# An attention and MLP kernel whose planned order is shifted by a table of 144 offsets, with five waits written out

## The chip, the cores and the metric

The kernel runs on one core of a Trainium2 chip. The metric is the device time of one execution in microseconds; several runs are made and their median is given. One more execution is recorded by the hardware profiler, and all times of single operations come from that one.

## The reference

Four layers work on x, 2048 rows of 640 numbers. Layers one and three are a local attention, layers two and four an MLP, each with its own layer norm and a residual; both attention layers share their weights, and so do both MLP layers.

```
x = x + A(layernorm(x), wqkv, wo)
x = x + B(layernorm(x), w1, b1, w2, b2)
x = x + A(layernorm(x), wqkv, wo)
x = x + B(layernorm(x), w1, b1, w2, b2)
```

A makes q, k and v for 32 heads of 20 numbers. Each position attends to itself and to the seven positions 2, 4, ... 14 before it (those before the start are masked), with a softmax over the eight, and a product with wo follows. B is a product from 640 to 1536, a gelu (tanh form) and a product back to 640. All is in float32.

## The kernel before

The rows are taken in four units of 512: even or odd positions (attention reaches only positions of the same parity), first or second half. A unit is four row tiles of 128. Two attention-and-MLP layers over four units make eight passes, numbered n = 0 to 7. The 32 heads are worked in four groups of eight heads; a group of a pass has the number G = 4n + g.

Products run on TensorE in float16. To keep float32's accuracy each operand is split into a high and a low half (the high half is a float16 copy, made by ScalarE, the low half is the rest, made by VectorE), and each product is three: high by high, high by low, low by high.

The steps of a pass, with their lines and the names that the texts use:

- Layer norm (from L520): statistics per row on VectorE (`sq`, L536 to L538), the power for 1/sqrt on GpSimd (`r`, L541), the normalized rows y on VectorE (L579), their high half on ScalarE (`yh`, L586) and low half on VectorE (`yl`, L588). They are transposed: in pass 0 on TensorE (`turn`, L468, with copies out of PSUM at L474 and L476), later by a DMA (`yT`, L593).
- qkv (L627): for each row tile t and group g one product `qkvp(n, t, g)` of 15 matmuls into one of three PSUM banks of the pool `ps`. ScalarE copies it out (`ev`, L633), and a DMA stores pairs of them (`put`, L639, 480 KB). Loads bring q, k and v of a group back in another layout (`inq`, `ink`, `inv`, L658).
- Attention of a group (L701 to L748) on VectorE: products of q and k (`qk`), sums over a head (`lg`), mask, maximum, difference (`lm`, `mx`, `sub`), the exponential on ScalarE (`e`, L716), sum and reciprocal (`s`, `rc`, `at`), products with v (`pv`) and their sums (`ad`, `o`). ScalarE makes the high half of the heads (`oh`, L746).
- Projection (L770): `wop(n, t, c)`, added to x by VectorE (`xh`, L776).
- MLP (function `mlp`, L807 to L849): hidden products `hp`, gelu, halves, output products.
- For the last units another MLP (`mlp_fast`) works with seven products of sums and differences of blocks (p1 to p7) instead of eight block products: its hidden products `hp` (L1021, one 320 KB load `c1` each, L1015) or `fp1`, gelu (L1027), sums and halves of h (`fs`, `fh`, `fl`, L1036 to L1041), products `fp` (L1084, their weights `fw` at L1067 and L1072, two loads of 160 KB), and the residual `fe` (L1103) with the store of the output (`done`, L1108). The sums of x that it needs are transposed by DMAs that ScalarE issues (`sT`, L515), and the sums of weights are prepared by `prep_sums` and `prep_late`.
- The weights of w1 and w2 are loaded once (`st`, L439, 320 KB), split (`hi` on ScalarE L413, `lo` on VectorE L414) and stored as float16 (`mw`, L454), while the first passes run. wqkv is split at the very start (`wq`, L413 and L414).

What sets the order is the class `Plan`. Every step is added with its engine, the steps it needs (`need`), what it gives (`give`), the buffers it uses (`use`) and a priority. `run` walks through the steps with an assumed duration for each, and at every point takes for each engine the step that can begin first; among equals the one of lowest priority number goes first. Buffers are handed out in the same walk, for example the three banks of `ps` and three buffers each of `c1` and `c2` (first and second kind of streamed weights). The result is one order for each engine; the program issues its instructions in that order, and an engine never overtakes. Nearly all DMAs are issued by SyncE, so they too go out in one order.

Of the kernel before, what the change touches and what calls it, by code (L numbers as in the profile page):

```python
# [14 lines left out]
S, D, H, DH, W, DIL, F = 2048, 640, 32, 20, 8, 2, 1536  # L15
# [52 lines left out]
LOP = {"sy": -460, "sa": -3}  # L68


class Plan:


# [24 lines left out]

    def add(self, eng, dur, prio, emit, need=(), give=(), use=(), table=None, move=0.0, lazy=False, spare=0.0,
            opens=0, beside=0, until=None):  # L100
        o = dict(eng=eng, dur=dur, prio=prio, emit=emit, need=need, give=give, use=use, table=table,
                 move=move, lazy=lazy, spare=spare, opens=opens, beside=beside, until=until, behind=None, ins=None, n=len(self.ops))
        self.ops.append(o)
        for u in use:
            if u not in self.users and u[0] in self.ORDERED and u not in self.line.setdefault(u[0], []):
                self.line[u[0]].append(u)
            self.users[u] = self.users.get(u, 0) + 1
# [133 lines left out]
def sliding_dilated_then_mlp_kernel(  # L241
# [245 lines left out]
    def sums_of_pairs(n, name, prio):  # L487
# [11 lines left out]
        for r in (2, 3, 0, 1):  # L499
# [12 lines left out]

            def turned(low=low, z=z, i=r % 2):
                v = tile_of(*sk)[:, :16 * HT2].rearrange("p (r c) -> p r c", c=HT2)
                nc.scalar.dma_start_transpose(v[:, 8 * z:8 * z + 8, i * P:(i + 1) * P], low().rearrange("p a c -> p (a c)"))  # L515

            dma_transpose(prio, turned, need=[("sl", n, r)], give=[("sT", n, r)], use=[hk, sk], by="act")

    def layernorm(n, prio, yk, twice):
        la, u = divmod(n, NU)  # L520
# [12 lines left out]
        for t in range(m if fast else 0):  # L533
            def stats(t=t):
                for i in range(2):
                    nc.vector.bn_stats(bn[:, t, 6 * i:6 * i + 6], x[u][:, t, i * D // 2:(i + 1) * D // 2])  # L536
                nc.vector.bn_aggr(bn[:, t, 12:14], bn[:, t, :12])
                return nc.vector.tensor_scalar_add(bn[:, t, 13:14], bn[:, t, 13:14], EPS)  # L538

            def rstd(t=t):  # L540
                nc.gpsimd.tensor_tensor(bn[:, t, 13:14], bn[:, t, 13:14], half[:, :1], op=OP.pow)  # L541

            dve(D, first(t), stats, need=[("x", la, u, t)], give=[("sq", name, t)], use=[lk], more=0.5)
            pool(0.5, prio, rstd, need=[("sq", name, t), "half"], give=[("r", name, t)], use=[lk])
        for t in range(0 if fast else m):
            act(D, prio, lambda t=t: nc.scalar.activation(junk, x[u][:, t], AF.Copy, scale=-1.0 / D,  # L546
# [313 lines left out]
    def prep_sums(j, prio):  # L860
# [5 lines left out]

        for z in range(2):
            dma(328, prio, lambda z=z: nc.sync.dma_start(parts()[0][:, z], B_w2[(j + z * HF) * P:(j + z * HF + 1) * P]),
                need=[("qkvp", N - 1, M - 1, NG - 1)], give=[("tr", j, z)], use=[key])

        def block(i):
            return parts()[0][:, i // 2, i % 2 * HD:(i % 2 + 1) * HD]
# [47 lines left out]
    def mlp_fast(at, b):  # L920
# [135 lines left out]
        for n, q in enumerate(PRODUCTS):  # L1056
            half, slot = (0, SLOT[q]) if SLOT[q] < 3 else (1, SLOT[q] - 3)
            for i in range(HF // 2):
# [17 lines left out]
                for t in range(2):  # L1076
# [14 lines left out]
                    else:  # L1091
                        prev = [p for p in PRODUCTS[:n] if BANKS[p] == BANKS[q]]
                        need += [("fe", b, prev[-1], t)] if prev else []
                    mm(6 * HD, 6, j, product, need=need, give=[("fp", b, q, i, t)], use=[wk, bk] + hks * (n in (0, NS - 1)))
            for t in range(2):
                bank = {"a": 0, "c": 2}[BANKS[q]] + t
                bk = (f"acc{bank}", (b, "a") if BANKS[q] == "a" else (b, "p2") if q == "p2" else (b, "c"))
# [91 lines left out]
```

## Time and profile before

| what | us |
| --- | --- |
| median of 3 runs | 1156.36 (1155.85 to 1156.84) |
| the profiled execution | 1155.75 |
| its span, first to last instruction | 1154.0 |
| TensorE (PE) busy | 1138.9 |
| VectorE (DVE) busy | 1067.8 |
| ScalarE (ACT) busy | 563.7 |
| GpSimd (POOL) busy | 158.1 |

The profiled execution's time is 1.75 us more than its span, and 0.61 us less than the median. Busy times of engines overlap, so they do not add up to the span. In a row of a timeline stand the start, the duration, the engine, the line, the operation with output and inputs, how many instructions are joined, and in brackets how long the engine was idle just before and what it waited for. In a row of waits stand the total, how often, and the longest. In a row of a stretch stand its bounds and length, the busy time and instructions of PE, weight loads, DVE, ACT and POOL, then the granted TensorE clock, the DMA share and GB/s. SPq rows are DMAs as SyncE issues them.

### The profile page before, as it was taken

Reading aid. Unit: us, or ns where it says so; the run is one execution under the profiler, and the core shown is the slowest. Engines: PE = TensorE matmul, PEld = TensorE weight load, DVE = VectorE, ACT = ScalarE, POOL = GpSimd, SP = SyncE. Lnnn points to the kernel's source line nnn. Section 1 sums busy time; section 2 is a strip of 40 time slices with the busy share of each in tenths; the row PEclk is TensorE's granted clock in tenths of the full one; section 3 lists DMA queues with packets and bytes.
Section 4 is the critical chain, followed back from the end, with each engine's and each line's share of the span. In section 5 each row is a group of like instructions: output and inputs, shape, how many; then the busy total and the mean of one; then the engine's idle time right before and its main releaser. Section 6 shows DMA issues by size and latency. Waiting matters only on the chain.

```text
span 1154.0 us, 17777 instructions
## 1 busy us (share of the span) xinstructions
PE 1138.9 (99%) x6952; PEld 647.5 (56%) x6952; DVE 1067.8 (93%) x1007; ACT 563.7 (49%) x985; POOL 158.1 (14%) x98
## 2 busy tenths in 40 slices
PE   8999999999999999999999999999999999999998
PEld 5444445577754565446555544556455546466786
DVE  7899999999999999999999999999998999988382
ACT  6475433645474438433636453357338342376260
POOL 1010001212111102101213001122410110200000
PEclk9999999999999999999999999999999999999999
DMA  9998999988976666846855774567678957688846
GB/s 283 286 346 252 253 352 298 283 280 272 250 215 186 196 187 162 238 160 171 193 196 177 189 216 164 192 183 178 184 232 262 318 176 212 197 205 225 222 121 188
DMA packets 256400, 256.73 MB, mean 222 GB/s; under 512 B 135916, under 2 KB 206908, under 8 KB 256316
## 3 DMA queue, kind: packets, MB, share of 16 engines
q1 hardware_dynamic: 252092, 254.55, 75.6%
q10 hardware_dynamic: 4224, 1.05, 0.5%
q8 instruction: 54, 0.88, 0.3%
q14 instruction: 30, 0.25, 0.1%
HBM read 175.64 MB, written 48.71 MB: 194 GB/s over the span
## 4 chain that ended last, share of the span: by engine, by line
PE 86%; DVE 8%; DMA 3%; issue 1%; ACT 1%; SPq 0%; DVEq 0%; ACTq 0%
PE ps L627 33%; PE ps L807 15%; PE acc L826 12%; PE ps L770 10%; PE acc L1084 6%; PE ps L1021 3%; PE acc L829 3%; PE acc L984 3%; DMA c<-mw 2%; DVE pr L701 2%; DVE sm L705 1%; DMA wq<-in_B_w_dram 1%; DVE wq L1036 1%; DVE pr L735 1%; DMA pr<-in_A_wqkv_dram 1%
## 5 line engine op out<-in xcount | busy, mean ns | idle before, releaser
L627 PE MATMUL ps<-wq,yT 128*128 128x480 f16 x1920 | 391.3, 366 | 0.6 <-DVE xf L776 0.4
L627 PEld LDWEIGHTS <-yT 128*128 128x128 f16 x1920 | 187.6, 98 | 200.9 <-DVE yT L474 0.8
L807 PE MATMUL ps<-yT,c 128*128 128x512 f16 (+1 forms) x1080 | 205.2, 344 | 0.0
L826 PE MATMUL acc<-c,act 128*128 128x512 f16 x720 | 200.2, 379 | 0.1
L701 DVE TENSOR_TENSOR pr<-qk 128x2560 f32<-128x2560 f32 (+1 forms) x44 | 176.5, 4014 | 2.1 <-DMA qk<-spill 2.0
L727 DVE TENSOR_TENSOR pr<-sm,v 128x2560 f32<-128x2560 f32 (+1 forms) x44 | 176.7, 4029 | 0.2
L705 DVE TENSOR_REDUCE sm<-pr 128x128 f32<-128x2560 f32 (+1 forms) x44 | 176.5, 4011 | 0.0
L807 PEld LDWEIGHTS <-c 128*128 128x128 f16 x1080 | 103.3, 98 | 86.3 <-DMA c<-mw 0.2
L829 PE MATMUL acc<-c,act 128*128 128x128 f16 x720 | 148.6, 219 | 0.1
L735 DVE TENSOR_TENSOR pr<-pr 128x1280 f32<-128x1280 f32 (+2 forms) x88 | 141.5, 1622 | 0.1
L633 ACT ACTIVATE ev<-ps 128x480 f32<-128x480 f32 x128 | 72.1, 564 | 139.1 <-PE ps L627 136.5
L770 PE MATMUL ps<-wo,yT 128*128 128x320 f16 x960 | 132.8, 299 | 1.2 <-ACT act L813 0.6
L563 POOL TENSOR_TENSOR ln<-ln,half 128x2 f32<-128x2 f32 (+1 forms) x30 | 65.3, 2179 | 398.8 <-ACT ln L560 398.8
L770 PEld LDWEIGHTS <-yT 128*128 128x128 f16 x960 | 93.7, 98 | 39.4 <-issue 2.0
L826 PEld LDWEIGHTS <-act 128*128 128x128 f16 x720 | 70.2, 98 | 81.3
L813 ACT ACTIVATE act<-ps,b 128x512 f32<-128x512 f32 (+1 forms) x72 | 44.1, 613 | 135.0 <-PE ps L807 125.3
L748 POOL TENSOR_TENSOR ohl<-o,ohl 128x640 f16<-128x640 f32 x24 | 43.7, 1822 | 386.5 <-DVE sm L718 123.0
L1084 PE MATMUL acc<-c,wq 128*128 128x320 f16 x630 | 93.8, 299 | 0.9 <-DVE wq L1036 0.7
L1021 PE MATMUL ps<-yT,c 128*128 128x512 f16 x360 | 80.4, 385 | 2.9 <-DMA c<-mw 2.6
L1084 PEld LDWEIGHTS <-wq 128*128 128x128 f16 x630 | 61.6, 98 | 25.6 <-DVE wq L1036 1.0
L829 PEld LDWEIGHTS <-act 128*128 128x128 f16 x720 | 68.3, 98 | 6.7 <-DVE act L818 0.3
L546 ACT ACTIVATE junk<-xf 128x640 f16<-128x640 f32 x56 | 41.0, 732 | 54.5 <-DVE xf L776 42.1
(136 smaller groups left out, 1115.6 us busy)
## 6 DMA issues: line engine op xcount, KB each, us to landing
c<-mw SPq DMA_DIRECT2D x180, 320.0 KB, 3.5
spill<-ev SPq DMA_DIRECT2D x64, 480.0 KB, 4.1
qk<-spill SPq DMA_DIRECT2D x32, 880.0 KB, 6.0
v<-spill SPq DMA_DIRECT2D x32, 880.0 KB, 4.9
c<-msp SPq DMA_DIRECT2D x36, 320.0 KB, 3.5
qk<-spill SPq DMA_DIRECT2D x32, 320.0 KB, 3.5
c<-mw SPq DMA_DIRECT2D x54, 160.0 KB, 3.0
mw<-c SPq DMA_DIRECT2D x24, 320.0 KB, 5.3
```

The source lines that it names most:

```text
L627: nc.tensor.matmul(ps, transposed(yk)[:, a * KD + k, t * P:(t + 1) * P], wq[:, b, k, g], start=j == 0, stop=j == 3 * KD - 1)
L633: act(3 * GC, -400 + n, lambda i=i, pk=pk, ek=ek: nc.scalar.activation(tile_of(*ek)[:, :, i], tile_of(*pk)[:, :3 * GC].rearrange("p (a c) ...
L701: return nc.vector.tensor_mul(pr(pk), w[:, HALO + m + t0:HALO + m + t0 + TH, None, :].to_broadcast([P, TH, W, GC]), windows(w, t0, [GC, W] ...
L705: dve(E, G - 0.7, lambda pk=pk, t0=t0: nc.vector.tensor_reduce(lg(t0, t0 + TH).rearrange("p t w h -> p (t w h)"), pr(pk).rearrange("p t w ...
L727: return nc.vector.tensor_mul(pr(vk).rearrange("p t w (h d) -> p t (w h) d", d=DH), lg(t0, t0 + TH).rearrange("p t w h -> p t (w h)")[:, : ...
L735: dve(TH * w * GC, G - 0.9, lambda vk=vk, w=w: nc.vector.tensor_add(pr(vk)[:, :, 0:w], pr(vk)[:, :, 0:w], pr(vk)[:, :, w:2 * w]), need=[la ...
L770: nc.tensor.matmul(tile_of(*pk)[:, :D // 2], transposed(yk)[:, a * KD + k, t * P:(t + 1) * P], wo[:, b, k, c * D // 2:(c + 1) * D // 2], s ...
L807: nc.tensor.matmul(tile_of(*pk)[:, :nt], tile_of(*ck)[:, a, k * P:(k + 1) * P], transposed(yk)[:, c * KD + k, t0 * P:t1 * P], start=i == 0 ...
L826: nc.tensor.matmul(acc[i], w, tile_of(*wk)[:, c, :BANK], start=e == 0 and (a, c) == PASS[0], stop=end, skip_group_check=True)
L829: nc.tensor.matmul(acc[4][:, i * P:(i + 1) * P], w, tile_of(*wk)[:, c, BANK:], start=e == 0 and i == t0 and (a, c) == PASS[0], stop=end, s ...
L1021: nc.tensor.matmul(tile_of(*pk), tile_of(*ck)[:, a, k * P:(k + 1) * P], transposed(yk)[:, c * KD + k, :], start=i == 0, stop=i == 3 * KD - 1)
L1084: nc.tensor.matmul(acc[bank][:, :HD], tile_of(*hk)[half][:, a, slot, t * P:(t + 1) * P], load()[:, z, c], start=q in FIRST and i == 0 and ...
```

## The change

The class `Plan` gets a table, NUDGE, of 144 entries. Its key is what a step gives, its value is added to the step's priority. Five waits are added: the DMA transposes of sums of x (`sT`) wait for all transposes of the normalized rows of their pass; the statistics of an attention pass wait for the normalized rows of the pass before; the loads of `prep_sums` wait for all 16 qkv products of the last pass and not for the last one alone; the buffers of h stay in use through the last but one of the seven products; and a store of the output waits for every product that adds to its block.

Lines after are the lines before plus 29 or 30 (L633 is L663, L1084 is L1114). The diff, with the table cut to the entries of the places below:

```diff
+NUDGE = {
+    ('x', 0, 0, 1): -8.7, ('x', 0, 0, 2): 162.1, ('x', 0, 0, 3): 41.6, ('sq', 0, 1): 41, ('wq', 0, 1): -266.3, ('sq', ('a', 0), 3): 184.1,
...
+    ('pv', 6, 1): -298.8, ('qk', 7, 0): 356.8, ('lg', 7, 1): 525.6, ('r', ('b', 1), 3): 74.8, ('vr', ('a', 2), 2): 73.3, ('qkvp', 2, 3, 2): -29.5,
...
+}
     def add(self, eng, dur, prio, emit, need=(), give=(), use=(), table=None, move=0.0, lazy=False, spare=0.0,
             opens=0, beside=0, until=None):
+        prio += NUDGE.get(give[0], 0.0)
...
-                nc.scalar.dma_start_transpose(v[:, 8 * z:8 * z + 8, i * P:(i + 1) * P], low().rearrange("p a c -> p (a c)"))
-
-            dma_transpose(prio, turned, need=[("sl", n, r)], give=[("sT", n, r)], use=[hk, sk], by="act")
+                return nc.scalar.dma_start_transpose(v[:, 8 * z:8 * z + 8, i * P:(i + 1) * P], low().rearrange("p a c -> p (a c)"))
+
+            dma_transpose(prio, turned, need=[("sl", n, r), *[("yT", name, t) for t in range(M)]], give=[("sT", n, r)], use=[hk, sk], by="act")
...
-            dve(D, first(t), stats, need=[("x", la, u, t)], give=[("sq", name, t)], use=[lk], more=0.5)
+            dve(D, first(t), stats, need=[("x", la, u, t)] + [("y", ("a", n - 1), t)] * (n > 0), give=[("sq", name, t)], use=[lk], more=0.5)
...
-                need=[("qkvp", N - 1, M - 1, NG - 1)], give=[("tr", j, z)], use=[key])
+                need=[("qkvp", N - 1, t, g) for t in range(M) for g in range(NG)], give=[("tr", j, z)], use=[key])
...
-                    mm(6 * HD, 6, j, product, need=need, give=[("fp", b, q, i, t)], use=[wk, bk] + hks * (n in (0, NS - 1)))
+                    mm(6 * HD, 6, j, product, need=need, give=[("fp", b, q, i, t)], use=[wk, bk] + hks * (n in (0, NS - 2, NS - 1)))
...
-                        need=[("fe", b, q, t)], give=[("done", u, i, d)])
+                        need=[("fe", b, p, t) for p in PRODUCTS if SENT[p] == SENT[q]], give=[("done", u, i, d)])
...
+    made = {}
     for o in plan.run():
         o["ins"] = o["emit"]()
+        made.update((k, o["ins"]) for k in o["give"])
+        for k in o["need"]:
+            if o["give"][0][0] == "sT" and k[0] == "yT":
+                tc.add_manual_dep(o["ins"].ins, made[k].ins.name, mybir.DependencyInfo(
+                    mybir.DependencyClass.Sync, mybir.DependencyReason.DATA), reason="order")
```

No instruction of arithmetic is added or removed; the order of the instructions differs on every engine. Three places follow.

**The start, VectorE.** Before, from the first row tile's statistics (`bn` is their buffer) to the third's; `wq` are low halves of wqkv, `y_80` and `hl_82` the first tile's normalized rows and their halves, `acc_95` a PSUM bank:

```order
L536 BN_STATS bn<-xf 128x6 x2
L537 BN_AGGR bn<-bn 128x2
L538 TENSOR_SCALAR bn<-bn 128x1
L414 SCALAR_TENSOR_TENSOR wq<-pr,wq 128x5x160
L579 TENSOR_SCALAR y_80<-xf,bn 128x640
L414 SCALAR_TENSOR_TENSOR wq<-pr,wq 128x5x160
L588 TENSOR_TENSOR hl_82<-y_80,hl_82 128x640
L414 SCALAR_TENSOR_TENSOR wq<-pr,wq 128x5x160
L474 COPY yT_70<-acc_95 128x5x128
L536 BN_STATS bn<-xf 128x6 x2
L537 BN_AGGR bn<-bn 128x2
L538 TENSOR_SCALAR bn<-bn 128x1
```

The same place now:

```order
L566 BN_STATS bn<-xf 128x6 x2
L567 BN_AGGR bn<-bn 128x2
L568 TENSOR_SCALAR bn<-bn 128x1
L566 BN_STATS bn<-xf 128x6 x2
L567 BN_AGGR bn<-bn 128x2
L568 TENSOR_SCALAR bn<-bn 128x1
L609 TENSOR_SCALAR y_80<-xf,bn 128x640
L444 SCALAR_TENSOR_TENSOR wq<-pr,wq 128x5x160
L618 TENSOR_TENSOR hl_82<-y_80,hl_82 128x640
L444 SCALAR_TENSOR_TENSOR wq<-pr,wq 128x5x160 x2
L504 COPY yT_70<-acc_95 128x5x128
```

The second row tile's statistics have moved from behind the copy of the first tile's transposed rows to ahead of the first y. SyncE loads that tile second instead of after the first three weight loads, and ScalarE makes the first tile's high half after one weight split instead of three.

**Pass 2's qkv products, ScalarE.** Before, from the evacuation of product (2, 0, 3) on; `ps_90`, `ps_91` and `ps_92` are the three banks, `c<-act` are high halves of weights of the MLP, `ohl_73` is the head copy, `sm_86` the exponential:

```order
L633 ACTIVATE ev<-ps_92 128x3x160
L633 ACTIVATE ev<-ps_90 128x3x160
L633 ACTIVATE ev<-ps_91 128x3x160
L633 ACTIVATE ev<-ps_92 128x3x160
L746 ACTIVATE ohl_73<-o_84 128x4x160
L633 ACTIVATE ev<-ps_90 128x3x160
L716 ACTIVATE sm_86<-sm_86 128x256
L413 ACTIVATE c_79<-act 128x640
L633 ACTIVATE ev<-ps_91 128x3x160
L413 ACTIVATE c_74<-act 128x640
```

Now, from the same evacuation on:

```order
L663 ACTIVATE ev<-ps_90 128x3x160
L663 ACTIVATE ev<-ps_91 128x3x160
L663 ACTIVATE ev<-ps_90 128x3x160
L443 ACTIVATE c_79<-act 128x640
L443 ACTIVATE c_74<-act 128x640
L776 ACTIVATE ohl_73<-o_84 128x4x160
L663 ACTIVATE ev<-ps_91 128x3x160
L663 ACTIVATE ev<-ps_90 128x3x160
L663 ACTIVATE ev<-ps_92 128x3x160
```

TensorE runs product (2, 3, 2) just ahead of (2, 0, 3), seven products earlier; it fills bank 92, which is evacuated only at the end of these rows. The evacuation of (2, 3, 0), the fourth of the rows before, now stands behind the splits c_79 and c_74 and the head copy. On SyncE the loads of these two splits have moved ahead of a load of v (880 KB), a `put` of 480 KB and a weight store of 320 KB, and the second of them ahead of one more `put`.

**Where the products of the last tiles mix, SyncE.** Before, from the load of `c1` number 84 on (`mw_108`; number 85 is `mw_114`, 86 is `mw_109`); the rows of 128x2x320 are half-blocks `fw`:

```order
L1015 DMA c_75<-mw_108 128x1280
L1072 DMA c_79<-mw_126 128x2x320
L1072 DMA c_79<-mw_127 128x2x320
L1015 DMA c_74<-mw_114 128x1280
L658 DMA v_69<-spill_147 128x1760
L1108 DMA out_dram<-xf 128x320 x2
L1072 DMA c_77<-mw_130 128x2x320
L1072 DMA c_77<-mw_131 128x2x320
L1015 DMA c_75<-mw_109 128x1280
L1108 DMA out_dram<-xf 128x320
```

Now:

```order
L1045 DMA c_75<-mw_108 128x1280
L1045 DMA c_74<-mw_114 128x1280
L688 DMA v_69<-spill_147 128x1760
L1138 DMA out_dram<-xf 128x320 x2
L1045 DMA c_76<-mw_109 128x1280
L1138 DMA out_dram<-xf 128x320
L1102 DMA c_77<-mw_126 128x2x320
L1102 DMA c_77<-mw_127 128x2x320
```

Load 86 (`mw_109`) has moved ahead of four half-blocks, and it goes into buffer c_76 instead of c_75. On TensorE the last two p3 products of the unit, which use c_76 before it, run ahead of hidden product 84 instead of behind it, and the last p4 product runs behind hidden product 85.

More of the change, by code (lines that the diff above doesn't have):

```diff
@@ L68 @@
 LOP = {"sy": -460, "sa": -3}
+NUDGE = {
[8 rows of a table added]
+    ('qkvp', 3, 3, 2): 31.2, ('qkvp', 3, 3, 3): 7.9, ('wop', 3, 3, 0): -748.4, ('qkvp', 4, 2, 0): -50.2, ('at', 18): 4.2, ('ad', 18, 0, 4): 266.2,
[8 rows of a table added]
+    ('sr', 3, 1): 292.5, ('out', 0, 3, 1): 52.4, ('hp', 4): 646.6, ('outh', 0, 0, 3): 31.8, ('out', 0, 3, 3): 2.5, ('outh', 0, 5, 2): 104.4,
+    ('outh', 0, 5, 3): 92.5, ('out', 0, 6, 2): 3.3, ('hp', 19): 8.3, ('outh', 0, 8, 3): 2.2, ('outh', 1, 4, 1): 2.1, ('out', 1, 11, 3): -176.9,
+    ('out', 2, 11, 1): 12.2, ('outh', 3, 0, 0): 234.1, ('outh', 3, 3, 3): 379.3, ('outh', 3, 9, 3): 417.2, ('xr', 3, 0): -142.9, ('x', 1, 3, 0): -137.5,
+    ('x', 1, 3, 1): -154.6, ('hlo', 64): 75.8, ('outh', 4, 6, 2): 30.3, ('out', 4, 8, 1): 3.5, ('out', 4, 8, 3): 0.6, ('hp', 69): 1.4, ('hp', 70): 0.7,
[4 rows of a table added]
+}
 class Plan:
```

18 rows, old and new, of the table NUDGE are left out of this document.

## Prediction

> **What bounds the kernel now.** I read the page's busy times and its chain first, then TensorE by stretches, then TensorE's waits, then the single rows at three places.
>
> ```profile
> PE 1138.9 (99%) x6952; PEld 647.5 (56%) x6952; DVE 1067.8 (93%) x1007; ACT 563.7 (49%) x985; POOL 158.1 (14%) x98
> PE 86%; DVE 8%; DMA 3%; issue 1%; ACT 1%; SPq 0%; DVEq 0%; ACTq 0%
> ```
>
> TensorE is busy for 1138.9 of 1154.0 us and the chain runs through it for 86%. The change adds and removes no matmul, so all that it can give is in the 15.1 us of idle time and in matmuls that run slowly; all that it can take is a new idle time. By stretches (length, then TensorE's busy time, with the granted clock and GB/s at the end of a row):
>
> ```profile
> 0.00:20.00 20.00, 14.33 (x128) 10.25 (x129) 13.31 (x31) 10.32 (x14) 3.02 (x12) 1.00 1.01 306
> 180.00:900.00 720.00, 718.16 (x4389) 400.47 (x4388) 702.44 (x559) 361.07 (x651) 125.51 (x66) 1.00 0.72 210
> 950.00:975.00 25.00, 24.34 (x177) 17.03 (x176) 24.58 (x27) 6.79 (x9) 1.40 (x1) 1.00 0.67 191
> 975.00:1000.00 25.00, 22.16 (x125) 12.40 (x124) 24.68 (x23) 4.66 (x6) 6.65 (x1) 0.93 0.73 216
> 1070.00:1090.00 20.00, 19.57 (x162) 15.49 (x160) 5.60 (x13) 4.38 (x11) 0.00 (x0) 1.00 0.88 255
> 1130.00:1154.00 24.00, 20.68 (x153) 14.68 (x150) 4.91 (x10) 0.00 (x0) 0.00 (x0) 0.98 0.55 162
> ```
>
> The idle time is 5.67 us in the first 20, 2.84 in 975 to 1000, 3.32 in the last 24 (the end, which the change leaves nearly as it is), and only 1.84 us in the 720 us between 180 and 900. So there is little to win in the middle, and three places matter. The waits behind these holes (total, times, longest):
>
> ```profile
> PE acc L468 <- ACT hl L586: 3.0, 2, 2.0
> PE ps L1021 <- DMA c<-mw: 2.6, 1, 2.6
> PE acc L468 <- DVE hl L588: 1.2, 3, 0.6
> PE acc L1084 <- DVE wq L1036: 0.7, 1, 0.7
> PE ps L1021 <- ACT ev L1027: 0.3, 1, 0.3
> PE acc L1084 <- DVE xf L1103: 0.3, 1, 0.3
> ```
>
> **The start.** TensorE, then VectorE:
>
> ```profile
> 9.79 0.45 PE L468 MATMUL acc<-ident,hl 128*128 128x128 f16 x5 [2.02 <-ACT hl L586]
> 11.04 3.72 PE L627 MATMUL ps<-wq,yT 128*128 128x480 f16 x15
> 15.69 0.45 PE L468 MATMUL acc<-ident,hl 128*128 128x128 f16 x5 [0.94 <-ACT hl L586]
> 16.71 0.73 PE L468 MATMUL acc<-ident,hl 128*128 128x128 f16 x10 [0.57 <-DVE hl L588]
> 17.67 0.45 PE L468 MATMUL acc<-ident,hl 128*128 128x128 f16 x5 [0.23 <-DVE hl L588]
> ...
> 11.81 0.87 DVE L536 BATCH_NORM_STATS2 bn<-xf 128x6 f32<-128x320 f32 x2
> 13.03 0.88 DVE L536 BATCH_NORM_STATS2 bn<-xf 128x6 f32<-128x320 f32 x2
> 14.26 0.60 DVE L579 TENSOR_SCALAR y<-xf,bn 128x640 f32<-128x640 f32 x1
> ```
>
> After the first product TensorE waits 0.94 + 0.57 + 0.23 = 1.74 us for the second and third row tiles to be normalized. VectorE makes the statistics of both only after the first tile's transposed copy: 11.81 to 13.03 for the second, then the third, then y at 14.26. The change loads the second tile ahead of the first weights and makes its statistics before the first y, when VectorE waits for weights anyway. So 13.03 − 11.81 = 1.22 us leave the chain to y. Nothing else there is shortened, so I take **−1.2**. The bounds are −1.74 (all three waits) and 0: the tile's load now stands ahead of the weight loads of the first product.
>
> **A held PSUM bank at 130 to 157 us.** ScalarE's rows, one stretch with its GB/s, TensorE's row, and the sizes of the loads:
>
> ```profile
> 144.77 0.74 ACT L746 ACTIVATE ohl<-o 128x640 f16<-128x640 f32 x1 [0.89 <-DVE o L739]
> 146.34 0.57 ACT L633 ACTIVATE ev<-ps 128x480 f32<-128x480 f32 x1 [0.83 <-PE ps L627]
> 152.69 0.74 ACT L413 ACTIVATE c<-act 128x640 f16<-128x640 f32 x1 [3.91 <-DMA act<-in_B_w_dram]
> 155.11 0.74 ACT L413 ACTIVATE c<-act 128x640 f16<-128x640 f32 x1 [1.22 <-DMA act<-in_B_w_dram]
> ...
> 143.80:155.10 11.30, 11.30 (x58) 5.48 (x56) 8.90 (x10) 3.00 (x6) 1.40 (x1) 1.00 1.07 345
> ...
> 127.66 32.56 PE L627 MATMUL ps<-wq,yT 128*128 128x480 f16 x160
> ...
> spill<-ev SPq DMA_DIRECT2D x64, 480.0 KB, 4.1
> v<-spill SPq DMA_DIRECT2D x32, 880.0 KB, 4.9
> mw<-c SPq DMA_DIRECT2D x24, 320.0 KB, 5.3
> ```
>
> A qkv product is 15 matmuls, 32.56 × 15 / 160 = 3.05 us; none waits here before. After the change the product (2,3,2) runs 21 us early and keeps one of the three banks until its evacuation, which still stands late on ScalarE. TensorE then alternates between two banks, so product (2,3,1) can start only when the evacuation of (2,3,0) is done. That one has moved behind two weight splits and the head copy (ohl). The product that the row at 146.34 evacuates has just ended; one more of 3.05 us fits, so (2,3,1) is due at 149.2, or 148.0 with the start's 1.2. The second of the two splits ran at 155.11 when its weights landed. In the new order of SyncE a store of 480 KB, the load of v (880) and a weight store (320) stand behind both split loads instead of ahead, and another 480 stands behind the second: 2160 KB. At 345 KB/us that is 6.3 us, so its weights land at about 148.8; split, copy and evacuation take 0.74 + 0.74 + 0.57 = 2.05, which makes 150.9 and a wait of 2.9 us. The other way, VectorE's softmax steps of this group are postponed to after the normalized rows, so the transposes that block SyncE's queue can start earlier, and the wait may be nothing. Bounds: 0, and with weights no earlier than before 155.11 + 2.05 − 148.0 = 9.2 us. I take **+2.0**, nearer to the sum of bytes than to nothing. The start's gain goes into this wait: a TensorE that comes earlier waits longer.
>
> **Late attention beside the product MLP, 947 to 977 us.** VectorE makes the low halves of h in another order (that of tile 5's first half ahead of tile 4's second half) and one residual of p7 before the second of p5. The three waits of 0.7, 0.3 and 0.3 us above (L1036, L1103, L1027) are what this can give, 1.3 at most. The first two are directly of these orders: 1.0, and I take **−0.9**; 0 at worst.
>
> **The load of c1 86, 988 us.** TensorE, one piece of the chain, SyncE, and two stretches:
>
> ```profile
> 989.75 3.40 PE L1021 MATMUL ps<-yT,c 128*128 128x512 f16 x15
> 995.72 5.53 PE L1021 MATMUL ps<-yT,c 128*128 128x512 f16 x17 [2.56 <-DMA c<-mw]
> ...
> 988.32 7.35 DMA c<-mw
> ...
> 981.41 1.18 SPq L1072 DMA_DIRECT2D c<-mw  x2
> 985.30 1.72 SPq L1072 DMA_DIRECT2D c<-mw  x2
> 988.32 0.33 SPq L1015 DMA_DIRECT2D c<-mw  x1
> ...
> 985.00:990.00 5.00, 5.00 (x30) 2.67 (x28) 4.75 (x5) 1.62 (x2) 0.00 (x0) 1.00 0.94 303
> 995.00:1000.00 5.00, 4.28 (x12) 1.62 (x13) 5.00 (x3) 0.00 (x0) 3.68 (x1) 0.66 0.13 52
> ```
>
> The load goes out at 988.32, when the product before last has freed its buffer, and lands 7.35 us later; TensorE waits 2.56 us. Then its matmuls run slowly: at the pace of the row at 989.75 (3.40 / 15 = 0.227 us) 17 would take 3.85 us and not 5.53, so 1.7 us go with a granted clock of 0.66. In all 4.26 us. After the change four half-blocks (160 KB each, the pairs at 981.41 and 985.30) stand behind this load; its buffer is the one of the last p3 product, which now runs ahead of the two hidden products. With 640 KB less ahead at 303 KB/us it lands 2.1 us earlier even if it went out no earlier; 0.45 us of waiting remain, and no slow matmuls. **−3.8**; bounds −4.26 and 0.
>
> [...]
>
> [...]
>
> **The rest.** The load for the last tile's next hidden product goes out one place earlier: of 20.00 − 19.57 = 0.43 us idle in 1070 to 1090 I take **−0.3**. In 180 to 900 the order changes at some sixty places, but TensorE idles there 1.84 us in all; I take 0, bounded by a gain of 0.9 (half of it). Of the five written waits four hold operations that already came in that order; that for the output stores stands on a queue that carries loads, which is a rival below.
>
> **Sum.** −1.2 + 2.0 − 0.9 − 3.8 − 0.3 = −4.2. Span 1154.0 − 4.2 = 1149.8; the profiled execution took 1155.75, so 1.75 lie outside: 1151.55. The median of the runs is 0.61 above that execution: **1152.2**.
>
> **Rivals.**
> *No wait at 148* (chance 0.30): SyncE reaches the weight loads early enough, or ScalarE has idle time for them; the 3.91 us idle ahead of the split speaks for weights as the only limit. Sum −6.2, 1150.2 us.
> *The hidden product's load gains nothing* (0.20): in SyncE's order an output store now stands right ahead of it, and that store waits for VectorE's residual of p3. If VectorE, 4.75 of 5.00 us busy at 985 to 990, comes to it late, the load goes out when it did. Without the −3.8 the sum is −0.4, 1156.0 us. The moved residual, two places earlier in VectorE's order, speaks against it. That the change does nothing because TensorE is at its floor ends at the same place.
> *The held bank costs more than all gains* (0.16), the slower side: the weights land as late as before, TensorE waits 9.2 us and loses 1.7 to the clock; 9.2 + 1.7 − 6.2 = +4.7, 1161.1 us. It is slower by over 0.2% when the wait passes 6.8 us, so when the second split's weights land after 148.0 + 6.8 − 2.05 = 152.8. For it speaks that the copy engines of this stretch move 345 KB/us without a pause; against it that 2160 KB are taken from ahead of the load.
>
> **How the numbers follow.** My forecast has the remaining 0.34. 0.2% of 1156.36 is 2.3 us, about what a measurement of this kernel can tell from no change. The forecast and the first rival are faster by more (0.64), the second is within (0.20), the third beyond (0.16). The low end takes every gain at its bound: −1.74 + 0 − 1.3 − 4.26 − 0.43 − 0.9 = −8.6, 1147.7. The high end is the point from which the third rival decides, 1158.7; what is left out is that rival.
>
> **What would show it.** TensorE's first product of the second row tile at 16.8 and not 17.96. A wait of TensorE (L657) for ScalarE's evacuation near 148 to 151, of 2 us, where none was; full clock after it. The wait for the load of c1 86 under 0.5 us, and 15 matmuls in 3.4 us behind it. Idle time in 180 to 900 within 1 us of 1.84. I am wrong if the wait at 148 is missing or passes 5 us, if a wait of over 2 us stands at the load, or if a wait of over 1.5 us appears elsewhere.

## The result, and the profile after

The changed kernel takes 1146.85 us (median of 6 runs, 1146.03 to 1148.29), the kernel before 1155.81 in the same comparison (6 runs, 1152.44 to 1156.84): a ratio of 0.993 with a 95% interval of 0.9914 to 0.9945. It is faster by 0.55 to 0.86%. The forecast was faster by 0.36% (4.2 of 1156.4 us); the gain is about twice that. The median lies 0.85 us below the low end of the forecast, 1147.7, in which every gain stood at its bound. The profiled execution spans 1145.0 us where that of before spans 1154.0.

Busy times and the chain, after:

```profile
PE 1136.1 (99%) x6952; PEld 648.3 (57%) x6952; DVE 1068.0 (93%) x1007; ACT 565.1 (49%) x985; POOL 138.5 (12%) x98
PE 95%; DVE 3%; DMA 1%; SPq 1%; ACT 0%; issue 0%; POOL 0%; ACTq 0%; DVEq 0%
```

The work is the same, but the chain now runs through TensorE for 95% and not 86%: it leaves TensorE less often to wait for another engine. TensorE's largest waits that are left (total, times, longest; lines are 30 higher than before):

```profile
PE acc L498 <- ACT hl L616: 2.8, 1, 2.8
PE acc L1143 <- POOL ident L415: 1.3, 1, 1.3
PE ps L800 <- DVE xf L806: 0.5, 1, 0.5
...
PE ps L1051 <- DMA c<-mw: 0.3, 1, 0.3
```

Of the 2.6 us for streamed loads of hidden products (now L1051) 0.3 are left, at another product, and the waits of the p products (L1114) are gone. No wait at the held PSUM bank (L657) has come. By stretches:

```profile
0.00:20.00 20.00, 15.37 (x131) 11.83 (x132) 14.04 (x31) 10.40 (x14) 4.10 (x12) 0.91 0.99 300
180.00:900.00 720.00, 719.52 (x4399) 401.49 (x4398) 704.71 (x555) 362.10 (x649) 106.25 (x66) 1.00 0.72 209
950.00:975.00 25.00, 24.99 (x185) 17.87 (x184) 24.42 (x29) 4.86 (x6) 1.40 (x1) 1.00 0.77 222
975.00:1000.00 25.00, 25.00 (x137) 13.18 (x135) 24.54 (x19) 7.72 (x10) 5.94 (x1) 1.00 0.78 235
1070.00:1090.00 20.00, 20.00 (x182) 17.57 (x181) 10.38 (x22) 10.44 (x22) 0.00 (x0) 1.00 0.56 171
```

Idle time against before: 5.67 to 4.63 in the first 20 us, 1.84 to 0.48 between 180 and 900, 0.66 to 0.01 and 2.84 to 0.00 between 950 and 1000, 0.43 to 0.00 near 1080.

At the start, TensorE before and after:

```profile
17.96 6.24 PE L627 MATMUL ps<-wq,yT 128*128 128x480 f16 x30
```

```profile
8.84 0.71 PE L498 MATMUL acc<-ident,hl 128*128 128x128 f16 x5 [2.85 <-ACT hl L616]
9.35 1.91 PE L1143 MATMUL acc<-ident 128*128 128x128 f16 x16
...
17.17 6.24 PE L657 MATMUL ps<-wq,yT 128*128 128x480 f16 x30
```

The first product of the second row tile begins at 17.17 and not at 17.96, so 0.8 us are gained. The 72 matmuls on `ident` (L1143), which only fill the start and which no later step reads, all ran ahead of the first transposes before; now 24 of them run behind, as the second row shows for 16. They fill part of what was idle time.

At the held bank the SyncE and ScalarE rows tell why nothing waits:

```profile
128.93 5.62 SPq L623 DMA_TRANSPOSE yT<-hl  x2
...
137.58 2.15 SPq L469 DMA_DIRECT2D act<-in_B_w_dram  x2
...
142.93 1.50 ACT L443 ACTIVATE c<-act 128x640 f16<-128x640 f32 x2
144.33 0.72 ACT L776 ACTIVATE ohl<-o 128x640 f16<-128x640 f32 x1
145.56 0.57 ACT L663 ACTIVATE ev<-ps 128x480 f32<-128x480 f32 x1 [0.51 <-PE ps L657]
```

The two loads go out from 137.58 on, where they went out at 145.90 and after 146.94 before: VectorE makes the low halves that the two transposes need from 128.05 on, and before from 131.98 on, so these leave SyncE by 134.6 and not at 142.1. Both splits run at 142.93 with no wait for weights. The evacuation of (2,3,0) starts at 145.56 and waits for TensorE itself. TensorE needs that bank when product (2,2,1) ends: the evacuation of (2,3,0) shows that (2,3,0) ended at 145.5, one more product is 3.05 us, so at 148.5; the bank is free at 146.1.

At the load of c1 86, SyncE and TensorE after:

```profile
981.30 0.45 SPq L1045 DMA_DIRECT2D c<-mw  x1
...
980.96 6.64 PE L1051 MATMUL ps<-yT,c 128*128 128x512 f16 x30
987.44 0.98 PE L1114 MATMUL acc<-c,wq 128*128 128x320 f16 x6
988.25 16.35 PE L1051 MATMUL ps<-yT,c 128*128 128x512 f16 x75
```

Call the time from the issue of a load to the moment at which its product is due the lead of the load. Here the load goes out at 981.30 and its product begins at 988.25 without a wait: a lead of 6.95 us. Before, it went out at 988.32 and was due when the product ahead of it ended, 989.75 + 3.40 = 993.15, a lead of 4.83.

### The profile page after: what moved, and what is told of

Same layout as the page of the kernel before. It is cut to its first block, busy times and chain, and to the rows that moved or that the text cites. A ratio compares the mean times of both kernels' runs of the same rounds, so it can differ in the third digit from the quotient of the medians.

```text
span 1145.0 us, 17774 instructions
## 1 busy us (share of the span) xinstructions
PE 1136.1 (99%) x6952; PEld 648.3 (57%) x6952; DVE 1068.0 (93%) x1007; ACT 565.1 (49%) x985; POOL 138.5 (12%) x98
## 4 chain that ended last, share of the span: by engine, by line
PE 95%; DVE 3%; DMA 1%; SPq 1%; ACT 0%; issue 0%; POOL 0%; ACTq 0%; DVEq 0%
PE ps L657 34%; PE ps L837 17%; PE acc L856 13%; PE ps L800 10%; PE acc L1114 9%; PE ps L1051 5%; PE acc L859 3%; PE acc L1014 3%; DVE pr L757 1%; DVE pr L765 1%; DMA c<-mw 1%; PE ps L1014 1%; DMA pr<-in_A_wqkv_dram 0%; SPq L789 0%; DMA wq<-in_B_w_dram 0%; PE acc L498 0%
## 5 line engine op out<-in xcount | busy, mean ns | idle before, releaser
L657 PE MATMUL ps<-wq,yT 128*128 128x480 f16 x1920 | 390.6, 366 | 0.0
L657 PEld LDWEIGHTS <-yT 128*128 128x128 f16 x1920 | 187.7, 98 | 199.9
L663 ACT ACTIVATE ev<-ps 128x480 f32<-128x480 f32 x128 | 72.2, 568 | 160.5 <-PE ps L657 146.6
L765 DVE TENSOR_TENSOR pr<-pr 128x2560 f32<-128x2560 f32 (+2 forms) x88 | 141.2, 1617 | 0.1
L800 PE MATMUL ps<-wo,yT 128*128 128x320 f16 x960 | 132.4, 299 | 0.5 <-DVE xf L806 0.5
L800 PEld LDWEIGHTS <-yT 128*128 128x128 f16 x960 | 93.7, 98 | 38.0 <-issue 0.6
L1114 PE MATMUL acc<-c,wq 128*128 128x320 f16 x630 | 93.1, 299 | 0.0
L593 POOL TENSOR_TENSOR ln<-ln,half 128x2 f32<-128x2 f32 (+1 forms) x30 | 45.8, 1526 | 376.4 <-ACT ln L590 376.4
L1051 PE MATMUL ps<-yT,c 128*128 128x512 f16 x360 | 78.8, 379 | 0.5 <-DMA c<-mw 0.3
L1114 PEld LDWEIGHTS <-wq 128*128 128x128 f16 x630 | 61.6, 98 | 24.5 <-issue 0.2
```

Source lines behind the costliest of these rows:

```text
L657: nc.tensor.matmul(ps, transposed(yk)[:, a * KD + k, t * P:(t + 1) * P], wq[:, b, k, g], start=j == 0, stop=j == 3 * KD - 1)
L663: act(3 * GC, -400 + n, lambda i=i, pk=pk, ek=ek: nc.scalar.activation(tile_of(*ek)[:, :, i], tile_of(*pk)[:, :3 * GC].rearrange("p (a c) ...
L765: dve(TH * w * GC, G - 0.9, lambda vk=vk, w=w: nc.vector.tensor_add(pr(vk)[:, :, 0:w], pr(vk)[:, :, 0:w], pr(vk)[:, :, w:2 * w]), need=[la ...
L800: nc.tensor.matmul(tile_of(*pk)[:, :D // 2], transposed(yk)[:, a * KD + k, t * P:(t + 1) * P], wo[:, b, k, c * D // 2:(c + 1) * D // 2], s ...
L1051: nc.tensor.matmul(tile_of(*pk), tile_of(*ck)[:, a, k * P:(k + 1) * P], transposed(yk)[:, c * KD + k, :], start=i == 0, stop=i == 3 * KD - 1)
L1114: nc.tensor.matmul(acc[bank][:, :HD], tile_of(*hk)[half][:, a, slot, t * P:(t + 1) * P], load()[:, z, c], start=q in FIRST and i == 0 and ...
```

## The experiments

All kernels hold the five written waits unless said otherwise. The plan is made anew for each table, so taking an entry out can move more than that entry; with each run stands how far the rows of its trace come in the same order.

**The waits alone.** The table is empty; every engine's order is that of the kernel before.

```diff
-NUDGE = { ... 144 entries ... }
+NUDGE = {}
```

> The five written waits with an empty table; the order of every engine is that of the kernel before. Theory (the gain is a sum of TensorE waits that the order removed, the written waits are free): within 1 us of the kernel before, with the same waits of TensorE, 2.5 us for the load of c1 86 among them. Rival (the written waits move the time by themselves): more than 2 us away, and a wait of TensorE that before does not have.

Measured: 1154.65 us (10 runs, 1151.27 to 1155.59) beside 1154.04 for before, a ratio of 0.999 (0.9972 to 1.0007). The written waits cost nothing that can be measured. But TensorE's waits are not those of before. The timeline around c1 86:

```profile
988.48 0.33 SPq L1045 DMA_DIRECT2D c<-mw  x1
...
989.92 8.25 PE L1051 MATMUL ps<-yT,c 128*128 128x512 f16 x36
```

The load of c1 86 goes out at 988.48, as late as before, and yet TensorE does not stop for longer than 0.2 us: the 36 matmuls in 8.25 us run through. In its place its waits show one at tile 7's first load, and two at other loads of hidden products, of 1.4 us at 1014 us and 0.5 at 933:

```profile
PE acc L1014 <- DMA c<-mw: 2.1, 1, 2.1
PE ps L1051 <- DMA c<-mw: 1.9, 2, 1.4
```

The part of the expectation that named the 2.5 us wait has failed: the order sets the lead, and the wait differs from one execution to the next.

**The kernel before once more**, for a second profile:

> The kernel before once more, for a second profile of its late stage. Theory of the lead: the load of c1 86 again goes out 4.8 us before its product is due, but lands earlier or later, so the wait of 2.56 us is not at the same place or not as long; waits of TensorE for streamed loads stand at one or two of the places near 995, 1014 and 1080, and the loss behind 900 us is again 6 to 8 us. Rival (the wait for c1 86 belongs to the order): again 2.2 us or more there.

Measured: 1154.2 us (8 runs, 1152.62 to 1158.27). Its rows:

```profile
988.45 0.33 SPq L1015 DMA_DIRECT2D c<-mw  x1
...
989.88 3.40 PE L1021 MATMUL ps<-yT,c 128*128 128x512 f16 x15
993.93 4.28 PE L1021 MATMUL ps<-yT,c 128*128 128x512 f16 x19 [0.65 <-DMA c<-mw]
```

The same load, sent 4.83 us ahead of need, makes TensorE wait 0.65 us here, at most 0.2 in the run above and 2.56 in the first profile. It lands 5.4, about 5.0 and 7.35 us after its issue. So the rival (the wait belongs to the order) has fallen. And the slow matmuls, which followed the 2.56 us, are in that one execution alone. Two more loads are late here: TensorE waits 0.68 us at 1014 us and 0.90 for tile 7's first load.

**The load behind fewer bytes.** Four half-blocks are held until the load of c1 86 has landed; TensorE's order is that of before up to 1018 us, where two p products now come ahead of the last projection.

```diff
-need=[("mw", r * HF + 2 * i + z, 1)], give=[("fw", b, m, z)], use=[wk])
+need=[("mw", r * HF + 2 * i + z, 1)] + [("c1", 86)] * ((b, m) in ((6, 3), (6, 5))), give=[("fw", b, m, z)], use=[wk])
```

> The order of the kernel before, with the written waits, and four half-block loads (fw 6,3 and 6,5) held until the load of c1 86 has landed; its buffer stays that of hidden product 84. Theory of the queue (640 KB ahead made the load late): it lands 2 us earlier after its issue, no wait over 0.3 us for it, the profile 2 to 4 us shorter than that of the kernel before. Theory of the lead: the lead stays 4.8 us, which is about what a load takes with little ahead, so the wait for it is small, but what was held back is late at its own product, and the median moves less than 2 us.

Measured: 1157.55 us (10 runs, 1152.83 to 1163.92) beside 1154.94, a ratio of 1.0026 (1.0005 to 1.0046). The profile is that of the slowest of the ten, 1163.92. In it c1 86 goes out at 992.78, and TensorE goes through product 86 without a wait:

```profile
994.21 9.01 PE L1051 MATMUL ps<-yT,c 128*128 128x512 f16 x41
```

but among its waits there are

```profile
PE acc L1114 <- DMA c<-mw: 3.2, 1, 3.2
PE acc L1114 <- DMA c<-msp: 2.9, 3, 1.6
```

The lead is again 994.21 + 3.40 − 992.78 = 4.83 us, and the load takes no longer than that. With the bytes ahead of it the same load took about 5.0 us in the run with the waits alone, so the bytes are not what decides. The waits of 6.1 us stand near 1075 to 1082 us, at loads for later p products; whether holding the four half-blocks made these late, or the moved order, this run does not show. The theory of the queue has failed: the time did not fall. The theory of the lead has the load right, and the time only in kind: 2.6 us by the medians, where it said less than 2.

**Parts of the table.** Three kernels keep a part of it: only the last 17 entries (from tile 5's sums on), all but these 17, and only two (the last p4 product of tile 5 and hidden product 84). The first and the third keep the order of before up to 950 and 980 us; the second keeps the changed order up to 916 us on SyncE and 944 on VectorE.

> The written waits and only the last 17 entries of the table (from tile 5's second layer of products on). Theory (places are independent): about -1.7 at 947 to 977, -4.4 at the load of c1 86, -0.6 at 1070 to 1090, +0.8 new waits near 1005, so 5 to 6 us faster than before, 1150 us. Rival (the early entries make VectorE and SyncE earlier, and the late places gain from that): less than 3 us faster.

> The written waits and all entries but the last 17. Theory: -0.8 at the start and -2.4 between 180 and 900, 3 us faster than before, and TensorE still waits some 2.5 us for the load of c1 86. Rival (the early entries carry the late gain): 6 us faster or more, the wait for the load under 1 us.

> The written waits and two entries alone: the last p4 product of tile 5 and hidden product 84, which puts the last p3 products ahead of hidden product 84 and gives the load of c1 86 their buffer. Theory (the load was late for its buffer and for what stood ahead of it on SyncE's queue): the load goes out 4 us or more before hidden product 86 is due, no wait there, full clock, 4 us faster than before. Rival (the gain there needs the other entries too, because half a pair of other loads still stands ahead of it): a wait of 1 us or more stays, under 3 us faster.

Measured: the last 17 alone 1191.07 us, a ratio of 1.0327 (1.0301 to 1.0353); the two alone 1165.52, 1.0103 (1.008 to 1.0126); all but the 17 1154.86, 1.0009 (0.999 to 1.0027). By their times the theory that each place has its gain to itself fails in all three. In one part it holds: without the 17 entries TensorE waits for the load of c1 86, which goes out at 985.13, a lead of 985.75 + 3.40 − 985.13 = 4.02 us.

```profile
985.75 3.40 PE L1051 MATMUL ps<-yT,c 128*128 128x512 f16 x15
991.18 9.02 PE L1051 MATMUL ps<-yT,c 128*128 128x512 f16 x41 [2.03 <-DMA c<-mw]
```

This kernel also has the early gain, and loses it behind 980 us (its numbers stand in the next part). The longest wait of the kernel with the last 17 alone:

```profile
PE acc L1114 <- DVE wq L1066: 36.0, 1, 36.0
```

With the early part of the order as before, VectorE takes attention steps from 953.78 us on, one after the other, and gets to these halves at 992.90; TensorE waits 36 us for them. In the changed kernel, with the same offsets of 32 and 63 on tile 5's sums of h (`fs` 5,4), the next attention step comes at 958.58, behind the halves. That the attention is further on there, and so not ready to go first, fits this; no run shows it by itself. The two entries alone do what they were expected to do at c1 86: three hidden products, 84 to 86, run through in 10.08 us.

```profile
990.12 10.08 PE L1051 MATMUL ps<-yT,c 128*128 128x512 f16 x45
```

But TensorE then waits for halves of h that VectorE makes too late:

```profile
PE acc L1114 <- DVE wq L1066: 6.0, 3, 4.7
```

An offset is not a move: what it moves depends on the rest of the table.

**Without the two entries** of the p4 product and hidden product 84, the rest of the table kept; the order is the changed one up to 976 us.

> The changed kernel without two entries of its table, those of the last p4 product of tile 5 and of hidden product 84; the order of all that comes before them stays. The load of c1 86 then gets the buffer of hidden product 84 again and stands behind four half-blocks. Theory (what counts is the time between the issue of a streamed load and its product: 4.8 us before, 7.0 us after, while the load takes 5 to 7.4): the lead falls back to about 5 us, a wait of 0 to 2.6 us returns there, with slow matmuls behind it when it is long, and the time is 1 to 4 us above the changed kernel's. Rival (the other moves of the late stage hold the gain): within 1 us of the changed kernel.

Measured: 1148.27 us (4 runs, 1146.87 to 1149.3); the changed kernel in the same comparison 1147.49. Its rows:

```profile
984.87 0.33 SPq L1045 DMA_DIRECT2D c<-mw  x1
...
986.30 3.40 PE L1051 MATMUL ps<-yT,c 128*128 128x512 f16 x15
990.19 4.06 PE L1051 MATMUL ps<-yT,c 128*128 128x512 f16 x18 [0.49 <-DMA c<-mw]
```

The lead falls back to 986.30 + 3.40 − 984.87 = 4.83 us, and a wait of 0.49 returns. 0.8 us for these entries is within the scatter, so the rival of the expectation holds (within 1 us) and its theory has the wait right and the time too high. This is the piece for which the prediction booked 3.8.

**The changed kernel once more.**

> The changed kernel once more, for its scatter and a second profile. Theory of the lead: its runs scatter less than those of the kernel before (1152.5 to 1160 in this study), about 1146 to 1148.5, and again no wait of TensorE over 0.7 us behind the first 20 us. Rival (the first profile was a lucky execution): runs up to 1152 and waits of 1 us or more in the late stage.

Measured: 1147.49 us (4 runs, 1147.15 to 1147.85), a ratio of 0.9936 (0.9921 to 0.9951). The stretches of both repeats, before (first three rows) and after:

```profile
0.00:100.00 100.00, 94.64 (x532) 49.33 (x533) 89.75 (x111) 61.90 (x117) 18.06 (x21) 1.00 0.93 294
100.00:900.00 800.00, 796.31 (x4774) 438.13 (x4773) 779.41 (x625) 395.19 (x706) 124.11 (x68) 1.00 0.76 219
900.00:1130.00 230.00, 226.91 (x1509) 145.53 (x1508) 194.43 (x265) 107.27 (x162) 17.30 (x9) 1.00 0.74 211
```

```profile
0.00:100.00 100.00, 96.40 (x536) 50.92 (x537) 90.95 (x112) 61.56 (x118) 11.87 (x20) 0.98 0.95 292
100.00:900.00 800.00, 798.96 (x4791) 439.80 (x4790) 783.53 (x625) 397.14 (x707) 105.47 (x69) 1.00 0.75 220
900.00:1130.00 230.00, 229.41 (x1539) 148.66 (x1538) 190.58 (x266) 106.16 (x161) 16.17 (x9) 1.00 0.77 214
```

Idle time of TensorE, before to after: 5.36 to 3.60, 3.69 to 1.04, 3.09 to 0.59 us. The gain is spread over the whole run and is not one wait; and what is left in the late stage is small in both profiles of the changed kernel. The times came as expected; a wait above the 0.7 us that I allowed stands at 867 us (0.95, for VectorE's residual).

Idle time is not all: for the same 6952 matmuls TensorE's busy time fell from 1138.9 to 1136.1 us between the first profiles, while the repeats have 1137.1 and 1137.2. So the gain is also counted by work, as the difference between the times at which the two kernels had streamed the same number of columns through TensorE, added up from the matmuls of the traces:

| gained by | first profiles, us | repeats, us |
| --- | --- | --- |
| 180 us | 0.8 | 0.8 |
| 900 us | 3.2 | 4.3 |
| the last matmul | 9.0 | 6.9 |

The seven profiles of kernels that keep the early entries (the one with late weights, below, is not counted) had 80% of this work done at 913.8 to 914.4 us, the three of the old order at 917.3 to 918.7. So the early part of the table is worth some 3 to 5 us up to there, also in the kernel without the last 17 entries, which is no faster in the end.

The late gain of the repeats, 2.6 us, is for the most part the three loads that were late before: 0.65 at c1 86, 0.68 at 1014 us and 0.90 at tile 7's first load, 2.2 in all. For that first load TensorE waited 0.4, 0.9 and 2.1 us in the three profiles of the old order and 1.7 without the last 17 entries, and in neither profile of the changed kernel.

**Which late entries count.** Without the last seven (tiles 6 and 7), without two of these (the sums `fs` 6,0,1 and 6,0,3, offsets 259.9 and 698.9), and without two others (products p5 and p7 of tile 6). TensorE keeps the changed order up to 1011 us in the first two, VectorE up to 997; in the third the order is kept up to 1057 us.

> The changed kernel without the last seven entries of its table (those of tiles 6 and 7 in the product MLP); the ten entries of tile 5 and of hidden product 84 stay, with the written waits. Theory of the lead: the load of c1 86 is in time, no wait of 0.7 us or more there; the first load of tile 7 (c1 7,0), issued 6.3 us ahead of its product in the changed kernel and 3.8 to 5.1 in the others, falls back to under 5 us, so 1 to 2.3 us of waiting stand at that product; 1 to 3 us above the changed kernel, 1148 to 1151. Rival (the last entries do nothing for the time): within 0.7 us of the changed kernel, no wait at that product.

> The changed kernel without the two entries that put the second and fourth sum of tile 6's first block of h behind the end of attention group 31 on VectorE (fs 6,0,1 and fs 6,0,3). Theory (finishing group 31 first lets the last projection go ahead of the last hidden products, and what follows has its data and its loads early): TensorE again waits 2 us or more for halves of h near 1044 and for loads near 1075, 4 to 7 us above the changed kernel, 1151 to 1154. Rival (the order of tile 6's last products decides): within 1.5 us of the changed kernel.

> The changed kernel without the two entries of tile 6's products p5 and p7; VectorE's order stays up to its last fifth. Theory of group 31: within 1.5 us of the changed kernel. Rival (the order of these products, with the buffer that it frees for tile 7's first load, decides): a wait of 1 us or more for loads near 1073, 3 us or more above the changed kernel.

Measured: without the seven 1155.61 us (1.0009, 0.9989 to 1.0028), without the two sums 1152.4 (0.9986, 0.9966 to 1.0005), without the two products 1147.26 (0.9946, 0.9926 to 0.9966). So the two sums are needed: without them the kernel is 5 us above the one without the two products, as expected, and what is left of the gain is not clear of the scatter, though 142 entries stay. The two products are not needed. Without the seven I had expected 1 to 3 us more than the changed kernel; by the two ratios to before it is 8, and TensorE has no wait for tile 7's first load, which was to be the cause. It waits 2.1 us for halves of h as below, and 1.9 for loads of p products. TensorE and VectorE without the two sums:

```profile
1015.91 16.47 PE L800 MATMUL ps<-wo,yT 128*128 128x320 f16 x120
1032.22 6.64 PE L1051 MATMUL ps<-yT,c 128*128 128x512 f16 x30
1045.85 5.65 PE L1114 MATMUL acc<-c,wq 128*128 128x320 f16 x28 [2.12 <-DVE wq L1066]
...
1004.89 0.81 DVE L769 TENSOR_TENSOR o<-pr 128x640 f32<-128x640 f32 x1
```

The same in the changed kernel:

```profile
1011.71 16.46 PE L800 MATMUL ps<-wo,yT 128*128 128x320 f16 x120
1028.01 9.88 PE L1051 MATMUL ps<-yT,c 128*128 128x512 f16 x45
...
999.04 0.81 DVE L769 TENSOR_TENSOR o<-pr 128x640 f32<-128x640 f32 x1
```

The two sums step aside for the end of the last attention group, so its output is done on VectorE at 999.9 and not at 1005.7. The last projection (L800) can start at 1011.7 and not at 1015.9, and three hidden products (45 matmuls) stand behind it instead of two. These cover VectorE's halves of the last block of h; with two, TensorE waits 2.12 us, and the granted clock from 1045 to 1050 us is 0.71 on average.

**Late weights at the held bank.** The two weight loads are put behind the load of v, made twice, and one store; the same order on TensorE, ScalarE and VectorE.

```diff
+    held = [order[at["st", ("m", 5, 1)]], order[at["st", ("m", 6, 0)]]]
...
+    order[i:i] = held
```

> The changed kernel with the loads of the two weight splits that stand ahead of the evacuation of product (2,3,0) put behind a load of v that is made twice, and behind one store: same order on TensorE, ScalarE and VectorE, weights later by some 6 us. Theory (the held bank is harmless only because the weights land in time): they land at 149 to 150, TensorE waits 3 to 4 us for the evacuation and then runs at half rate for a while, 5 us more than the changed kernel, 1152 us. Rival (the third bank or the slack of 2.2 us covers it): under 1 us more.

Measured: 1158.5 us (5 runs, 1156.63 to 1158.96), 11 us above the changed kernel in the same comparison.

```profile
155.13 10.15 PE L657 MATMUL ps<-wq,yT 128*128 128x480 f16 x37 [7.20 <-ACT ev L663]
...
153.26 0.74 ACT L443 ACTIVATE c<-act 128x640 f16<-128x640 f32 x1 [0.32 <-DMA act<-in_B_w_dram]
```

The weights landed later than I had expected (153.2 and not 149 to 150), and the mechanism is as described: 7.2 us of waiting, then half clock (0.50 from 155 to 160 us, 0.98 from 160 to 165). Counted by work 9.8 of the 11 us stand there, and most of the rest comes between 290 and 350 us; the cause of that part stays open. The bank is harmless only because its weights come in time.

No run pointed to a version faster than the changed kernel: each part of the table that I took out left it equal or slower.

## Why the prediction was right, and where it was wrong

The direction and the reason at large held: TensorE's work stays, and the gain is in its waits. Step by step:

- **Start, −1.2.** Right in kind, −0.8 in size. The sign was the first product of the second row tile at 16.8; it came at 17.17 (before 17.96), and at 16.72 in the repeat (before 17.55). The idle time of the first 20 us fell by more, from 5.67 to 4.63 and from 5.36 to 3.60, but 24 matmuls on `ident` moved into it, and for 3.41 us there the granted clock is at half (0.50 from 8.57 to 11.98 in the first profile). The term knew of neither. The wait ahead of the first transposed tile went from 2.02 to 2.85 in the first profiles and from 1.70 to 2.02 in the repeats.
- **Held bank, +2.0.** Wrong, 0.0, and by the prediction's own sign, since a missing wait at 148 was to show it wrong. The step that failed was "nearer to the sum of bytes than to nothing": I held the time at which SyncE reaches the loads, and counted only the bytes ahead. SyncE reached them 8.3 us earlier. Its two transposes begin 4.2 us earlier (128.93 and not 133.11), as VectorE's low halves come earlier; their issue takes 3.4 us less (5.62 and not 9.00); and what stands between them and the loads takes 0.8 less. I had named the earlier transposes and given them too little weight; it was the first rival's case. The late weights show that the mechanism was real: with the second split at 153.26 the prediction's sum gives 153.26 + 2.05 − 148.0 = 7.3 us, and 7.20 was measured. For the clock the sum puts nothing on a wait of 2.0 us, and no run shows that this holds in general: of two waits of 2.02 us at the start one had full clock behind it and one half. The third rival's 1.7 us for the clock is the loss measured once, behind 2.56 us; in the run with late weights 9.8 us were lost by work, 2.6 more than the wait of 7.20.
- **947 to 977, −0.9.** Right for the first profile, where the idle time of 950 to 975 fell by 0.65 us. But the repeat of before and the run with the waits alone have no idle time between 950 and 975 either (25.00 of 25.00 us busy). Only a wait of 0.3 us at 977, for a residual, stands in all three profiles of the old order. The rest belonged to one execution.
- **Load of c1 86, −3.8.** Right for the one execution that I had, wrong as a price of the order. The same lead of 4.8 us cost 2.56 us once, 0.65 in the repeat, at most 0.2 with the waits alone and 0.49 without the two entries, and a lead of 4.0 cost 2.03; the 1.7 us of slow matmuls came once. I took one execution's bad luck for a property of the program.
- **1070 to 1090, −0.3.** The three profiles of the old order have 0.43, 0.90 and 2.15 us there, at tile 7's first load, and both of the changed kernel none. The term was right, and sized by the smallest of the three.
- **180 to 900, 0 ± 0.9.** Wrong, beyond its bound. The idle time fell by 1.4 us in the first profiles and by 2.65 in the repeats (there from 100 to 900); by work the gain is 2.4 and 3.5. I took "little idle time" for "nothing to win". One piece that both profiles of before have is a projection: 120 matmuls (L770) from 649.25 on take 16.82 us and a wait of 0.41 for VectorE's residual follows at 669.78; the changed kernel's take 16.46 (from 646.42 on), with no wait.
- **Not in the sum at all:** the order of VectorE at the end of the last attention group. It decides how many hidden products are left to cover VectorE's halves. It is a wait that the new table would have without two of its entries, 5 us; so it explains why these are needed, and not a part of the difference to before.

The size came out at twice the forecast (9.0 us of span, and 6.9 in the repeats, where 4.2 were forecast). In the first profiles 2.0 of the 4.8 that are missing are the +2.0 that was not there, 2.4 are the middle, and 0.4 are left for the start and the late stage together. That the late stage came near its −5.0 there (5.8 by work) is luck: in the repeats it gave 2.6. How the late gain is divided among the entries stays open: parts of the table make another plan, so they can't be added up.

## What to carry to other kernels

Where one engine is busy 99% of the span, read the lead of each streamed load (issue to need) beside the times that this load takes to land in several profiles, and not the one wait that a profile happens to show. In the three profiles of the old order c1 86 had a lead of 4.8 us, landed after 7.4, 5.4 and 5.0 us and was late each time; c1 84 had 4.7, landed after 3.1 to 3.4 and was never late. A short lead is no fault by itself. That longer leads alone would help is not shown, as no run lengthened a lead and left the rest in place. An entry in a table of priorities has no worth of its own; test it by taking it out of the full table, not by using it alone. Count a gain by the work done up to a point, beside the idle time. Before a reordering is charged with a new wait, check whether the queue that feeds it has also become earlier.

## What the runs showed of the hardware

TensorE's granted clock fell to half at some waits of 2.0 to 2.9 us and not at others. At the start of the changed kernel it is at half for 3.41 us around the end of a wait of 2.85 us:

```profile
8.57:11.98 3.41, 3.14 (x30) 3.14 (x31) 3.34 (x5) 2.44 (x4) 0.00 (x0) 0.50 1.09 370
```

In the kernel before it is at half for as long behind the 2.56 us at c1 86 (0.50 from 995.93 to 999.34). Behind the 2.12 us of the run without the two sums it is 0.71 on average from 1045 to 1050 us and 0.95 from 1050 to 1055, which makes 3.4 us at half. The 2.1 us wait of the run with the waits alone left the clock at full:

```profile
1080.00:1085.00 5.00, 4.72 (x44) 4.25 (x45) 0.42 (x1) 1.93 (x5) 0.00 (x0) 1.00 0.68 246
```

Even two waits of 2.02 us at the start differ: in the first profile of before the clock is full behind it (1.00 from 9 to 14 us), in the repeat of the changed kernel it is 0.71 from 8 to 12 us and 0.86 from 12 to 16. What decides between the two, no run shows.

The issue of a DMA transpose on SyncE is not short: two took 5.62 us after (from 128.93 on) and 9.00 before (from 133.11 on), and the next DMA on SyncE went out at 134.65 and 142.16. In the whole trace of before, single ones of L593 took 1.3 to 6.2 us.

```profile
133.11 9.00 SPq L593 DMA_TRANSPOSE yT<-hl  x2
```
